# Sequence 0 of an attention-and-gate kernel: one pair of heads moved from float32 products to float16 parts, and one product of the first keys with two query blocks

## The chip, the cores and the metric

The kernel runs on one core of one Trainium2 chip. The core has five engines that run side by side and meet only through semaphores: TensorE (PE: matrix products, and its weight loads, PEld), VectorE (DVE), ScalarE (ACT), GpSimd (POOL) and SyncE (SP, which in this kernel issues every DMA). The metric is the device time of one execution in microseconds; lower is better. Times quoted as "the median" are over several executions; the profile is of one execution.

## The reference, cut to what matters

Eight sequences (B = 8) of 576 tokens, eight heads (H = 8) of width 64. Each head does causal softmax attention and a read of a linear memory; both are mixed by a gate per head. The result, 4608 x 512, goes through a two-layer net with the gate h * clip(h + 3, 0, 6) / 6.

```python
scores = scale * np.matmul(q, k.transpose(0, 1, 3, 2))
scores = np.where(causal, -1000000000.0, scores)
a = np.exp(scores - scores.max(-1, keepdims=True)); a /= a.sum(-1, keepdims=True) + 1e-09
local = np.matmul(a, v)
q_p = phi(q)                                   # elu(q) + 1
mem_out = (q_p @ M_prev) / (q_p @ z_prev + 1e-06)
attn = g * mem_out + (1 - g) * local
...
h = x @ w_in
out = (h * np.clip(h + 3.0, 0.0, 6.0) / 6.0) @ w_out
```

## The kernel before

**Tiling.** A sequence's 576 tokens are five query blocks (four of 128 and one of 64). Heads go in four pairs (p = 0 to 3). A `Unit` (L325) is one head of one pair for a group of query blocks; the groups are `UNITS` (L321): blocks 0 and 1 together (u = 0), then 2, 3 and 4 alone. A sequence has 32 units, in the order u, pair, head; unit t of sequence 0 with u = 0 has t = 0 to 7, so the last pair has t = 6 and 7, then 14 and 15, 22 and 23, 30 and 31. A unit does `scores` (PE: keys times queries, one product per key block j up to the query block, and the causal mask by another product), `reduce` (a maximum: DVE at L371, ACT for block 0, then an all-reduce over partitions on POOL at L373), `sub` (DVE, L379), `exp` (ACT, L386), `pv` (PE: the values, and the memory) and, after a pair's second head, `combine`.

**Two arithmetics.** For sequences 1 to 7 each operand is split into a float16 high and low part. `prep_steps` (L168) does that for a pair: three loads into staging tiles (tag stg, three buffers), sums of absolute values on ACT and an all-reduce on POOL, scales, then for k, q, phi(q) and v a `split` (L160: ACT writes the high part, DVE the low one). For k and phi(q) `stack` (L213) moves the parts by SBUF-to-SBUF DMAs, four for each, so that high and low lie on partitions 0 to 63 and 64 to 127; `do_q` issues four such DMAs too. The parts of k, q, phi and phi(q) come from a pool of three buffers (tag hl). `mem_steps` (L288) does the same for a sequence's memory. A score is then two products of float16 (L354, L355) and one mask (L361), a value product is three (L423 to L425), a memory product two per head (L427); POOL makes the high part of the weights (L390), DVE the low one (L398), and `combine` uses four ACT instructions a block (L455, L456) and one DVE add (L457).

For sequence 0 all four pairs are used as they are loaded, in float32 (`nat`): `nat_load` brings a pair in two parts, `nat_phi` makes phi(q) on ACT and DVE, a score is one float32 product on 64 partitions (L350), the mask is done by products with `selm` and `neg2` (L358), a value product is one float32 product (L416), the memory product of a pair is one (L418), and `combine` multiplies and adds on DVE (L446, L448). Each float32 product is two PE instructions in the trace, one of float16 is one.

**Slots.** Six slots (NSLOT) hold what a pair needs. The pairs of sequence 0 use slots 0 to 3, slots 4 and 5 are first the landing place for weights; `selm` and `neg2` lie at the tail of slot 3.

**The weights.** w_in and w_out come as 64-bit numbers, 16 loads of 1 MB (`w_load`). `w_decode` turns one into float32: ACT (L643), DVE (L644, L645), and a sum of absolute values on ACT (L646) that writes over the landing place, after which the next load may be issued into it. Block 0 of the net (256 tokens, `NNAT`) runs in float32 on these (L537, L563); then the weights are split in place (`w_split`), and the other 17 blocks run in float16 parts (L542 to L544, L565 to L567). Block 0 needs the rows of query blocks 0 and 1 of sequence 0 from all four pairs, which PE transposes (L524).

**The order.** `LOADS` (L40) is the order of the first loads: kind 0 and 1 are the two parts of a pair of sequence 0, 2 a weight load, 3 the memory. `B_T` (L41) says at which t the second part of each pair's phi is made. Every piece of work is given a due number (`due`, L736, `at`); a planner at compile time simulates the engines and lays down a fixed order for each engine from these numbers. At run time each engine goes through its own order and waits where an operand isn't there.

Of the kernel before, what the change touches and what calls it, by code (L numbers as in the profile page):

```python
# [28 lines left out]
SA = 256.0  # L29
TINY = 2.0 ** -40  # L30
NSLOT = 6
NNAT = 1

X_T = 10
# [2 lines left out]
W_AFTER = [3, 4, 5, 5, 6, 6, 7, 7] + [7] * 8  # L37
PSS, PSO = 3, 2

LOADS = ((0, 0), (3, 0), (0, 1), (0, 2), (0, 3), (2, 0), (2, 1), (1, 0), (1, 1), (2, 2), (1, 2), (1, 3), (2, 3))  # L40
B_T = (2, 3, 4, 5)  # L41
OF = (0,)
RMAX_STEPS = 3.0
LEAD = 40
# [24 lines left out]
def kernel(ctx, tc, qT, kT, v, mz, beta, w_in, w_out, out):  # L69
# [48 lines left out]
    for i in range(NSLOT):  # L118
        sizes = [2 * NB * P, 4 * S, 2 * S, NB * 2 * 129]
        whole = const.tile([P, sum(sizes) + 2], F16, name=f"slot{i}")  # L120
        at = 0
        for lst, n, pat, kw in zip((kst, qhl, qps, vst), sizes,
                                   ["p (h s) -> p h s", "p (x h s) -> p x h s", "p (h s) -> p h s",
                                    "p (t h e) -> p t h e"],
                                   [dict(h=2), dict(x=2, h=2), dict(h=2), dict(t=NB, h=2)]):
            lst.append(whole[:, at:at + n].rearrange(pat, **kw))
            at += n
        if i < NP:
            w32 = whole.bitcast(F32)
            nat.append(dict(q=w32[:, 0:S], k=w32[:, S:S + NB * P], qp=w32[:, S + NB * P:2 * S + NB * P],  # L130
                            v=w32[:, 2 * S + NB * P:2 * S + NB * P + NB * 130]
                            .rearrange("p (t h e) -> p t h e", t=NB, h=2)))
        else:
            raw.append(whole[:, 0:4096])
        if i == NP - 1:

            free = whole.bitcast(BF16)[:, 2 * (2 * S + NB * P + NB * 130):]
            selm = free[:, 0:2 * P].rearrange("p (a k) -> p a k", a=2)
            neg2 = free[:, 2 * P:3 * P].rearrange("p (a q) -> p a q", a=2)

    def at(step):

        tc.cur_priority = int(round(step * 1000))
# [24 lines left out]
    def prep_steps(b, p):  # L168
        sl = (NP * b + p) % NSLOT
        st = {}  # L170

        def pad(dst, value):
            if NP * b + p < NP + NSLOT:
# [20 lines left out]
        def scale():  # L194
            amr = st["amr"]
            ACT.activation(amr[:, 3:4], amr[:, 0:1], AF.Copy, bias=1.0)
            s, i = scales(amr, 4, TS, f"{b}_{p}")
            st["s"] = s
            scal = small.tile([P, 4], F32, name=f"scal_{b}_{p}", tag="scal", bufs=8)
            DVE.scalar_tensor_tensor(scal[:, 0:1], i[:, 0:1], 0.125, i[:, 1:2], op0=ALU.mult, op1=ALU.mult)  # L200
            DVE.memset(scal[:, 2:3], SA * 1e-9)
            ACT.activation(scal[:, 3:4], s[:, 3:4], AF.Copy, scale=mem[b]["eps1"])
            coef = mem[b]["coef"][:, 2 * p:2 * p + 2]
            ACT.activation(coef[:, :, 0], omg[:, 2 * p:2 * p + 2], AF.Copy, scale=i[:, 2:3])
            eps = scal[:, 2:4].unsqueeze(1).broadcast_to([P, 2, 2])
            esc = scal[:, 0:1]
            slots[b, p] = dict(sl=sl, esc=esc, coef=coef, eps=eps)
# [67 lines left out]
    def nat_mem():  # L275
        m = p2.tile([P, H * (D + 1)], F32, name="m_nat", tag="mz")
        DVE.memset(m, 0.0)
        m = m.rearrange("p (j h e) -> p j h e", h=2, e=D + 1)
        for r in range(2):
            SP.dma_start(m[D * r:D * r + D, :, r], mz[0].rearrange("d (j h) e -> d j h e", h=2)[:, :, r])  # L280
        coef = small.tile([P, H, 2], F32, name="coef_0", tag="coef", bufs=2)
        DVE.tensor_copy(coef[:, :, 0], omg)
        DVE.tensor_copy(coef[:, :, 1], gate)
        mem[0] = dict(t=m, coef=coef)
# [3 lines left out]
    def mem_steps(b):  # L288
        st = {}

        def load():
            t = st["t"] = stg.tile([P, NB * P], F32, name=f"stm_{b}", tag="stg")
            m = st["m"] = t[:, 0:H * (D + 1)].rearrange("p (h e) -> p h e", e=D + 1)
            for r in range(2):
                SP.dma_start(m[D * r:D * r + D], mz[b])

        def absmax():
            am = small.tile([P, 2], F32, name=f"amm_{b}", tag="amm", bufs=2)
            amr = st["amr"] = small.tile([P, 2], F32, name=f"ammr_{b}", tag="ammr", bufs=2)
            m = st["m"]  # L300
            abs_sum(am[:, 0:1], m[:, :, 0:D])
            abs_sum(am[:, 1:2], m[:, :, D:])
            POOL.partition_all_reduce(amr, am, P, RMAX)

        def conv():
            s, i = scales(st["amr"], 2, TS, f"m{b}")
            t = p2.tile([P, 2, H, D + 1], F16, name=f"mz_{b}", tag="mz")
            m = st["m"]
            split(t[:, 0, :, 0:D], t[:, 1, :, 0:D], m[:, :, 0:D], s[:, 0:1])
            split(t[:, 0, :, D:], t[:, 1, :, D:], m[:, :, D:], s[:, 1:2])  # L310
            coef = small.tile([P, H, 2], F32, name=f"coef_{b}", tag="coef", bufs=2)
            DVE.tensor_scalar(coef[:, :, 1], gate, s[:, 1:2], i[:, 0:1], op0=ALU.mult, op1=ALU.mult)
            eps1 = small.tile([P, 1], F32, name=f"eps1_{b}", tag="eps1", bufs=2)
            DVE.tensor_scalar_mul(eps1, s[:, 1:2], 1e-6)
            mem[b] = dict(t=t, s=s, coef=coef, eps1=eps1)

        return [load, lambda: None, absmax, conv]

# [6 lines left out]
    class Unit:  # L325
        def __init__(self, b, u, p, h):
            self.b, self.u, self.p, self.h = b, u, p, h
            self.blocks = []
            c = mcol = 0
            for i in UNITS[u]:  # L330
                self.blocks.append((i, rows[i], c, mcol))
                c += (i + 1) * rows[i]
                mcol += rows[i]
            self.n, self.m = c, mcol
            self.id = f"{b}_{u}_{p}_{h}"

        def scores(self):
            h = self.h
            if self.b == 0:
                t = nat[self.p]  # L340
            else:
                sl = slots[self.b, self.p]["sl"]
            sT = self.sT = ps_s.tile([P, 512], F32, name=f"sT_{self.id}", tag="sT")
            for i, nq, c0, _ in self.blocks:
                q0 = i * P
                for j in range(i + 1):
                    o = sT[:, c0 + j * nq:c0 + (j + 1) * nq]
                    if self.b == 0:
                        r = slice(D * h, D * h + D)
                        PE.matmul(o, t["k"][r, j * P:(j + 1) * P], t["q"][r, q0:q0 + nq],  # L350
                                  start=True, stop=j < i)
                    else:
                        kk = kst[sl][:, h, j * P:(j + 1) * P]
                        PE.matmul(o, kk, qhl[sl][:, 0, h, q0:q0 + nq], start=True, stop=False)  # L354
                        PE.matmul(o, kk, qhl[sl][:, 1, h, q0:q0 + nq], start=False, stop=j < i)  # L355
                    if j == i and self.b == 0:
                        for a in range(nq // D):
                            PE.matmul(o[:, a * D:(a + 1) * D], selm[r, a, :], neg2[r, a, :],  # L358
                                      start=False, stop=a == nq // D - 1)
                    elif j == i:  # L360
                        PE.matmul(o, ident16, negm[:, 0:nq], start=False, stop=True)  # L361
# [22 lines left out]
        def exp(self):  # L384
            a = self.a[:, 0:self.n]
            self.exp_ins = ACT.activation(a, a, AF.Exp, scale=slots[self.b, self.p]["esc"], bias=LN_SA)  # L386
            if self.b == 0:
                return
            self.ah = p2.tile([P, 512], F16, name=f"ah_{self.id}", tag="ah")
            POOL.affine_select(self.ah[:, 0:self.n], a, pattern=[[0, self.n]], compare_op=ALU.is_ge,  # L390
                               fill=0.0, base=1, channel_multiplier=0)

        def lo(self):
            if self.b == 0:
                return
            self.al = p2.tile([P, 512], F16, name=f"al_{self.id}", tag="al")
            n = self.n
# [1 line left out]

        def pv(self):  # L400
            b, p, h = self.b, self.p, self.h
            mt = mem[b]["t"]
            for i, nq, c0, _ in self.blocks:
                if h == 0:
                    if b == 0 and i in OF and i < 2:
# [5 lines left out]
                o, om = g[0:nq, h, 0, :], g[0:nq, h, 1, :]  # L411
                qs = slice(i * P, i * P + nq)
                cs = [slice(c0 + j * nq, c0 + (j + 1) * nq) for j in range(i + 1)]
                if b == 0:
                    for j in range(i + 1):
                        PE.matmul(o, self.a[:, cs[j]], nat[p]["v"][:, j, h, :], start=j == 0, stop=j == i)  # L416
                    if h == 1:
# [274 lines left out]
    DVE.memset(bias_g, TG / 2.0)  # L692
    DVE.memset(half, 0.5)
    DVE.memset(amx, 0.0)
    for p in range(NP):
        nat_pads(p)
    DVE.memset(nat_eps[:, 0:1], SA * 1e-9)
    DVE.memset(nat_eps[:, 1:2], 1e-6)
# [4 lines left out]
    for x, n in LOADS:  # L703
        if x < 2:
            nat_load(n, x)
        elif x == 2:
            w_load(n)
        else:
            nat_mem()
    am1 = const.tile([P, 8], F32, name="am1")  # L710
    am2 = const.tile([P, 8], F32, name="am2")
    for p in range(NP):
        nat_phi(p, 0)

    def w1_split():
# [45 lines left out]
    for t in range(NU + 2):  # L761
        if t < NU:
            u = units[t]
            if t % upb == 0 and u.b + 1 < B:
# [3 lines left out]
                for p, ks in enumerate(PREP_AT if t else PREP_AT_0):  # L768
                    for f, k in zip(ps[p], ks):
                        plan.setdefault(t + k, []).append(f)  # L770
        for p in range(NP):
            if t == B_T[p]:
                at(due(t) + PO)
                nat_phi(p, 1)
# [64 lines left out]
```

## Time and profile before

| what | us |
|---|---|
| median of 3 runs | 1101.2 (1100.18 to 1104.09) |
| the profiled execution, its own time | 1104.08 |
| its span, first to last instruction | 1102.4 |
| PE busy in the span | 1071.24 |
| DVE busy | 893.04 |
| ACT busy | 788.96 |
| POOL busy | 405.18 |

The profiled execution is at the upper end of the three runs; 1.7 us of its time lie outside its span. An engine's busy time is the union of its instructions. On PE the ends of matmuls are modelled, so what PE can do is read from the distance between the starts of like instructions rather than from their durations. The rows that matter are shown with the prediction.

### The profile page before, as it was taken

To read this page: it belongs to the slowest core of one execution; us is meant where nothing else is said; L and a number is where in the kernel's file an instruction comes from. 1 tells how busy PE (TensorE), PEld (TensorE's weight loads), DVE (VectorE), ACT (ScalarE), POOL (GpSimd) and SP (SyncE) were. 2 spreads that over 40 slices of the span, in tenths; PEclk is the share of its full clock that TensorE was granted. 3 is DMA by queue.
4 is the path that set the end of the run, shared out by engine and by line. 5 is a ranking of instruction groups with operands and counts; after the bars stand their busy time and mean duration, and the time that the engine had idled before them with its cause. 6 is when DMAs were issued, how large, how long until landed. Compare 5 with 4: busy or idle time off the path is not lost.

```text
span 1102.4 us, 28691 instructions
## 1 busy us (share of the span) xinstructions
PE 1071.2 (97%) x10728; PEld 788.6 (72%) x10728; DVE 893.0 (81%) x2350; ACT 789.0 (72%) x1884; POOL 405.2 (37%) x544
## 2 busy tenths in 40 slices
PE   7999999899999999999999999999999999999998
PEld 6888758586767776776768686768686858685664
DVE  5989779899899979998989896999699868792321
ACT  4778769778888878788877887778687857563322
POOL 2322123445455434533344533453244433350000
PEclk9999999999999999999999999999999999999999
DMA  8835452334333432443433432332432230101100
GB/s 251 313 110 174 108 148 78 77 85 102 102 97 97 98 106 78 117 92 101 103 102 47 136 99 51 81 102 76 128 82 68 52 77 14 29 10 31 30 10 20
DMA packets 101467, 101.38 MB, mean 92 GB/s; under 512 B 50256, under 2 KB 80976, under 8 KB 101328
## 3 DMA queue, kind: packets, MB, share of 16 engines
q1 hardware_dynamic: 101328, 99.56, 33.6%
q8 instruction: 84, 1.38, 0.6%
q14 instruction: 55, 0.45, 0.1%
HBM read 48.14 MB, written 9.44 MB: 52 GB/s over the span
## 4 chain that ended last, share of the span: by engine, by line
PE 39%; DVE 18%; ACT 5%; issue 5%; DMA 4%; POOL 1%; SPq 1%; DVEq 0%; ACTq 0%; POOLq 0%
PE po L565 6%; PE po L567 6%; PE po L566 6%; PE ph L542 5%; PE ph L543 5%; PE ph L544 5%; DVE rm L371 3%; DVE a L379 3%; DVE al L398 3%; DVE r L551 2%; DVE g L553 2%; PE sT L354 1%; PE sT L355 1%; PE o L425 1%; PE o L423 1%
## 5 line engine op out<-in xcount | busy, mean ns | idle before, releaser
L373 POOL PARTITION_ALL_REDUCE mb<-rm x256 | 253.9, 992 | 354.5 <-DVE rm L371 249.8
L542 PE MATMUL ph<-x,W 128*128 128x256 f16 x1088 | 296.6, 273 | 3.0 <-DMA x<-W 2.2
L543 PE MATMUL ph<-x,W 128*128 128x256 f16 x1088 | 296.6, 273 | 0.0
L544 PE MATMUL ph<-x,W 128*128 128x256 f16 x1088 | 296.6, 273 | 0.0
L565 PE MATMUL po<-W,g 128*128 128x512 f16 x544 | 206.2, 379 | 5.0 <-ACT ot L573 3.5
L567 PE MATMUL po<-W,g 128*128 128x512 f16 x544 | 206.2, 379 | 0.9 <-DVE g L553 0.9
L566 PE MATMUL po<-W,g 128*128 128x512 f16 x544 | 206.2, 379 | 0.0
L390 POOL TENSOR_SCALAR_AFFINE_SELECT ah<-a 128x384 f16<-128x384 f32 (+2 forms) x224 | 138.3, 619 | 183.0 <-ACT a L386 124.3
L386 ACT ACTIVATE a<-a,scal 128x384 f32<-128x384 f32 (+2 forms) x224 | 141.0, 631 | 63.1 <-DVE a L379 54.1
L379 DVE TENSOR_TENSOR a<-sT,mb 128x128 f32<-128x128 f32 (+3 forms) x320 | 148.3, 479 | 25.6 <-POOL mb L373 19.7
L398 DVE TENSOR_TENSOR al<-a,ah 128x384 f16<-128x384 f32 (+2 forms) x224 | 135.5, 605 | 10.7 <-POOL ah L390 9.9
L371 DVE TENSOR_REDUCE rm<-sT 128x128 f32<-128x256 f32 (+3 forms) x256 | 135.0, 527 | 8.3 <-ACT rm L369 3.8
L551 DVE SCALAR_TENSOR_TENSOR r<-r,ph 128x512 f32<-128x512 f32 x136 | 92.0, 677 | 52.5 <-ACT r L550 51.9
L550 ACT ACTIVATE r<-ph,bias_g,gsc 128x512 f32<-128x512 f32 x136 | 106.4, 783 | 33.2 <-PE ph L544 29.4
L355 PE MATMUL sT<-slot 128*128 128x128 f16 (+1 forms) x840 | 126.7, 210 | 0.0
L354 PE MATMUL sT<-slot 128*128 128x128 f16 (+1 forms) x840 | 124.2, 210 | 1.9 <-DVE a L379 1.4
L542 PEld LDWEIGHTS <-W 128*128 128x128 f16 x1088 | 106.4, 98 | 18.1 <-issue 3.0
L423 PE MATMUL o<-slot,ah 128*128 128x65 f16 (+1 forms) x840 | 116.1, 196 | 3.2 <-POOL ah L390 1.6
L543 PEld LDWEIGHTS <-W 128*128 128x128 f16 x1088 | 106.3, 98 | 15.7 <-issue 1.1
L424 PE MATMUL o<-slot,ah 128*128 128x64 f16 (+1 forms) x840 | 115.2, 195 | 0.0
L455 ACT ACTIVATE x<-o,cf 128x64 f32<-128x64 f32 (+1 forms) x280 | 88.0, 314 | 37.4 <-DVE cf L442 37.2
L544 PEld LDWEIGHTS <-W 128*128 128x128 f16 x1088 | 106.3, 98 | 11.7
(157 smaller groups left out, 2297.3 us busy)
## 6 DMA issues: line engine op xcount, KB each, us to landing
slot<-q SPq DMA_DIRECT2D x112, 144.0 KB, 2.5
out<-ot SPq DMA_DIRECT2D x36, 256.0 KB, 2.0
stv<-vn SPq DMA_DIRECT2D x28, 320.0 KB, 3.5
W<-w_in SPq DMA_DIRECT2D x8, 1024.0 KB, 11.2
slot<-w_out SPq DMA_DIRECT2D x8, 1024.0 KB, 5.0
stq<-qT SPq DMA_DIRECT2D x28, 288.0 KB, 3.1
stk<-kT SPq DMA_DIRECT2D x28, 288.0 KB, 3.2
slot<-k SPq DMA_DIRECT2D x112, 72.0 KB, 2.0
```

Source lines behind the costliest of these rows:

```text
L371: DVE.tensor_reduce(rm[:, m0:m0 + nq], src.rearrange("p (t q) -> p q t", q=nq), axis=AX.X, op=ALU.max)
L373: POOL.partition_all_reduce(mb[:, 0:self.m], rm[:, 0:self.m], P, RMAX)
L379: DVE.tensor_tensor(a[:, c0:c0 + w].rearrange("p (t q) -> p t q", q=nq), self.sT[:, c0:c0 + w].rearrange("p (t q) -> p t q", q=nq), self.m ...
L386: self.exp_ins = ACT.activation(a, a, AF.Exp, scale=slots[self.b, self.p]["esc"], bias=LN_SA)
L390: POOL.affine_select(self.ah[:, 0:self.n], a, pattern=[[0, self.n]], compare_op=ALU.is_ge, fill=0.0, base=1, channel_multiplier=0)
L398: DVE.tensor_tensor(self.al[:, 0:n], self.a[:, 0:n], self.ah[:, 0:n], op=ALU.subtract)
L542: PE.matmul(ph[:, m], wh, f["xh"][:, c], start=c == 0, stop=False)
L543: PE.matmul(ph[:, m], wh, f["xl"][:, c], start=False, stop=False)
L544: PE.matmul(ph[:, m], wl, f["xh"][:, c], start=False, stop=c == 3)
L565: PE.matmul(po, gh[:, m, ts], W2[:, m, 0:512], start=m == 0, stop=False)
L566: PE.matmul(po, gh[:, m, ts], W2[:, m, 512:], start=False, stop=False)
L567: PE.matmul(po, gl[:, m, ts], W2[:, m, 0:512], start=False, stop=m == 15)
```

## The change

The last pair of sequence 0 (p = 3) is no longer used in float32: it is loaded, split and stacked as the pairs of the later sequences are, and its units take the float16 branch in all but `combine`. Its `prep_steps` (that is, the steps after the load) and those of a `mem_steps(0)` are issued with the units t = 1 to 4, by the tables `PREP_0` and `MEM_0`, and their loads stand fourth in `LOADS` (kind 4). The memory of sequence 0 is therefore loaded twice, once in float32 for pairs 0 to 2 and once to be split; its landing place and its parts, and `selm` with `neg2`, lie in the unused tails of slots 0, 2 and 1.

For the pairs that stay in float32, the unit of blocks 0 and 1 does key block 0 in one product with 256 queries; before, there were two products with 128 queries each.

```diff
+NATP = 3
-LOADS = ((0, 0), (3, 0), (0, 1), (0, 2), (0, 3), (2, 0), (2, 1), (1, 0), (1, 1), (2, 2), (1, 2), (1, 3), (2, 3))
-B_T = (2, 3, 4, 5)
+LOADS = ((0, 0), (3, 0), (0, 1), (4, 3), (0, 2), (2, 0), (2, 1), (1, 0), (1, 1), (2, 2), (1, 2), (2, 3))
+B_T = (2, 3, 4)
+
+PREP_0 = (0, 0, 1, 1, 2, 2, 2, 3, 4, 4)
+MEM_0 = (0, 0, 1, 2)
...
-        if i < NP:
+        if i < NATP:
...
-        if i == NP - 1:
-
-            free = whole.bitcast(BF16)[:, 2 * (2 * S + NB * P + NB * 130):]
+        free = whole[:, 2 * (2 * S + NB * P + NB * 130):]
+        if i == 0:
+            m16_raw = free.bitcast(F32)[:, 0:H * (D + 1)]
+        elif i == 2:
+            m16 = free[:, 0:2 * H * (D + 1)].rearrange("p (x h e) -> p x h e", x=2, h=H)
+        elif i == 1:
+
+            free = free.bitcast(BF16)
             selm = free[:, 0:2 * P].rearrange("p (a k) -> p a k", a=2)
...
+        mk = b or "split"
...
-            ACT.activation(scal[:, 3:4], s[:, 3:4], AF.Copy, scale=mem[b]["eps1"])
-            coef = mem[b]["coef"][:, 2 * p:2 * p + 2]
+            ACT.activation(scal[:, 3:4], s[:, 3:4], AF.Copy, scale=mem[mk]["eps1"])
+            coef = mem[mk]["coef"][:, 2 * p:2 * p + 2]
...
+            t = stg.tile([P, NB * P], F32, name=f"stm_{b}", tag="stg")[:, 0:H * (D + 1)] if b else m16_raw
...
+            t = p2.tile([P, 2, H, D + 1], F16, name=f"mz_{b}", tag="mz") if b else m16
...
+            self.nat = b == 0 and p < NATP
...
-                    if self.b == 0:
-                        r = slice(D * h, D * h + D)
+                    if self.nat and self.u == 0 and j == 0:
+
+                        if i == 0:
+                            PE.matmul(sT[:, 0:2 * P], t["k"][r, 0:P], t["q"][r, 0:2 * P], start=True, stop=False)
+                    elif self.nat:
                         PE.matmul(o, t["k"][r, j * P:(j + 1) * P], t["q"][r, q0:q0 + nq],
                                   start=True, stop=j < i)
...
-                    if j == i and self.b == 0:
+                    if j == i and self.nat:
...
-            if self.b == 0:
+            if self.nat:
                 return
             self.ah = p2.tile([P, 512], F16, name=f"ah_{self.id}", tag="ah")
...
-            mt = mem[b]["t"]
+            mt = mem[b if self.nat else b or "split"]["t"]
...
-                if b == 0:
+                if self.nat:
...
-    for p in range(NP):
+    for p in range(NATP):
         nat_pads(p)
...
+        elif x == 4:
+            prep0 = prep_steps(0, n)
+            mem0 = mem_steps(0)
+            prep0[0]()
+            mem0[0]()
...
-    for p in range(NP):
+    for p in range(NATP):
         nat_phi(p, 0)
...
-        for p in range(NP):
+        for fs0, ks in ((mem0, MEM_0), (prep0, PREP_0)):
+            for f, k in zip(fs0[1:], ks[1:]):
+                if k == t:
+                    at(due(t))
+                    f()
+        for p in range(NATP):
             if t == B_T[p]:
```

`scores`, `exp`, `lo` and `pv` test `self.nat` now; `combine` keeps its test `b == 0`, so the last pair still goes through L446 and L448 there.

More of the change, by code (lines that the diff above doesn't have):

```diff
@@ L132 @@
                             .rearrange("p (t h e) -> p t h e", t=NB, h=2)))
-        else:
+        elif i >= NP:
             raw.append(whole[:, 0:4096])
-        if i == NP - 1:
-            free = whole.bitcast(BF16)[:, 2 * (2 * S + NB * P + NB * 130):]
+        free = whole[:, 2 * (2 * S + NB * P + NB * 130):]
[5 more added lines that the diff above has]
+            free = free.bitcast(BF16)
             selm = free[:, 0:2 * P].rearrange("p (a k) -> p a k", a=2)
@@ L280, in nat_mem @@
             SP.dma_start(m[D * r:D * r + D, :, r], mz[0].rearrange("d (j h) e -> d j h e", h=2)[:, :, r])
-        coef = small.tile([P, H, 2], F32, name="coef_0", tag="coef", bufs=2)
+        coef = small.tile([P, H, 2], F32, name="coef_n", tag="coef", bufs=3)
         DVE.tensor_copy(coef[:, :, 0], omg)
@@ L291, in load @@
         def load():
-            t = st["t"] = stg.tile([P, NB * P], F32, name=f"stm_{b}", tag="stg")
-            m = st["m"] = t[:, 0:H * (D + 1)].rearrange("p (h e) -> p h e", e=D + 1)
+            t = stg.tile([P, NB * P], F32, name=f"stm_{b}", tag="stg")[:, 0:H * (D + 1)] if b else m16_raw
+            m = st["m"] = t.rearrange("p (h e) -> p h e", e=D + 1)
             for r in range(2):
@@ L306, in conv @@
             s, i = scales(st["amr"], 2, TS, f"m{b}")
-            t = p2.tile([P, 2, H, D + 1], F16, name=f"mz_{b}", tag="mz")
+            t = p2.tile([P, 2, H, D + 1], F16, name=f"mz_{b}", tag="mz") if b else m16
             m = st["m"]
@@ L310, in conv @@
             split(t[:, 0, :, D:], t[:, 1, :, D:], m[:, :, D:], s[:, 1:2])
-            coef = small.tile([P, H, 2], F32, name=f"coef_{b}", tag="coef", bufs=2)
+            coef = small.tile([P, H, 2], F32, name=f"coef_{b}", tag="coef", bufs=3)
             DVE.tensor_scalar(coef[:, :, 1], gate, s[:, 1:2], i[:, 0:1], op0=ALU.mult, op1=ALU.mult)
@@ L314, in conv @@
             DVE.tensor_scalar_mul(eps1, s[:, 1:2], 1e-6)
-            mem[b] = dict(t=t, s=s, coef=coef, eps1=eps1)
+            mem[b or "split"] = dict(t=t, s=s, coef=coef, eps1=eps1)
         return [load, lambda: None, absmax, conv]
@@ L338, in scores @@
             h = self.h
-            if self.b == 0:
+            if self.nat:
                 t = nat[self.p]
+                r = slice(D * h, D * h + D)
             else:
@@ L386, in exp @@
             self.exp_ins = ACT.activation(a, a, AF.Exp, scale=slots[self.b, self.p]["esc"], bias=LN_SA)
-            if self.b == 0:
+            if self.nat:
                 return
@@ L393, in lo @@
         def lo(self):
-            if self.b == 0:
+            if self.nat:
                 return
@@ L413, in pv @@
                 cs = [slice(c0 + j * nq, c0 + (j + 1) * nq) for j in range(i + 1)]
-                if b == 0:
+                if self.nat:
                     for j in range(i + 1):
```

## The prediction

> **What bounds the kernel now.** I read the head of the page first, for the share of each engine, then the windows view with a stretch for each stage.
>
> ```profile
> span 1102.4 us, 28691 instructions
> PE 1071.2 (97%) x10728; PEld 788.6 (72%) x10728; DVE 893.0 (81%) x2350; ACT 789.0 (72%) x1884; POOL 405.2 (37%) x544
> ```
>
> ```profile
> 0.00:20.00 20.00, 14.91 (x79) 13.58 (x79) 10.40 (x62) 7.05 (x17) 5.82 (x14) 1.00 0.80 238
> 20.00:40.00 20.00, 16.54 (x76) 14.93 (x76) 16.71 (x46) 14.27 (x28) 5.46 (x4) 1.00 1.00 330
> 40.00:61.00 21.00, 20.88 (x90) 18.42 (x89) 16.64 (x44) 17.69 (x36) 6.61 (x8) 1.00 0.51 198
> 61.00:140.00 79.00, 79.00 (x486) 62.07 (x485) 69.60 (x174) 59.09 (x109) 17.33 (x21) 1.00 0.46 140
> 140.00:163.00 23.00, 20.52 (x104) 10.63 (x102) 15.85 (x43) 15.95 (x33) 6.62 (x6) 0.93 0.57 147
> 163.00:1102.40 939.40, 919.39 (x9905) 669.00 (x9903) 763.82 (x1985) 674.90 (x1663) 363.35 (x492) 1.00 0.30 76
> ```
>
> PE is idle for 31.2 us in all (1102.4 - 1071.2), and 8.5 of these lie in the first 40 us. From 40 us on PE is the bound, so a microsecond of PE work that goes from sequence 0 after that is a microsecond off the end, if nothing new makes PE wait. From 20 to 40 us the DMA share is 1.00 at 330 GB/s: the front is paced by loads. DVE is no light load either, 69.60 of 79 us in the fourth stretch.
>
> Second, the price of a PE instruction: the timeline of PE, read from start to start of neighbouring groups.
>
> ```profile
> 57.24 1.65 PE L350 MATMUL sT<-slot 64*128 64x128 f32 x6
> 58.69 0.31 PE L358 MATMUL sT<-slot 64*128 64x64 bf16 x2
> 58.92 1.54 PE L416 MATMUL o<-slot,a 128*128 128x65 f32 x6
> 60.26 0.74 PE L418 MATMUL o<-m_nat,slot 128*128 128x130 f32 x2
> 60.80 5.50 PE L537 MATMUL ph<-x,W 128*128 128x256 f32 x20
> ...
> 69.78 5.45 PE L537 MATMUL ph<-x,W 128*128 128x256 f32 x24
> ...
> 80.43 1.16 PE L350 MATMUL sT<-slot 64*128 64x128 f32 x8
> 81.42 0.22 PE L358 MATMUL sT<-slot 64*128 64x64 bf16 x2
> ...
> 99.69 1.00 PE L416 MATMUL o<-slot,a 128*128 128x65 f32 x8
> 100.53 0.44 PE L418 MATMUL o<-m_nat,slot 128*128 128x130 f32 x2
> 100.90 1.16 PE L350 MATMUL sT<-slot 64*128 64x128 f32 x8
> ```
>
> Before 60.8 us a float32 score instruction takes (58.69 - 57.24)/6 = 0.242 us, after it (81.42 - 80.43)/8 = 0.124; a value instruction (60.26 - 58.92)/6 = 0.223, then (100.53 - 99.69)/8 = 0.105. So PE runs at half pace until about 61 us and at full pace afterwards, though the windows give a granted clock of 1.00 in both. The step comes when the first long run of float32 products of the net starts (60.80).
>
> **The change part by part.** *PE work of the last pair.* Two heads; blocks 0 to 2 (t = 6, 7, 14, 15) have 12 products in the slow stretch, block 3 has 8 and block 4 has 10 in the fast one. The float16 forms stand in the timeline of sequence 1:
>
> ```profile
> 156.50 0.22 PE L361 MATMUL sT<-negm,ident 128*128 128x128 bf16 x1
> ...
> 157.23 0.22 PE L361 MATMUL sT<-negm,ident 128*128 128x128 bf16 x1
> ```
>
> ```profile
> 163.54 0.19 PE L423 MATMUL o<-slot,ah 128*128 128x65 f16 x1
> ...
> 163.93 0.27 PE L544 MATMUL ph<-x,W 128*128 128x256 f16 x1
> ```
>
> From the first to the second row there are 13 steps, 0.056 us each; from the third to the fourth 12, 0.033 each. Their price at the slow pace has no row: at least these, at most double, as for every float32 form; I take double (0.113 and 0.065).
>
> - Slow, a product: 2 x 0.242 + 2 x 0.223 = 0.93 becomes 2 x 0.113 + 3 x 0.065 = 0.42, so 0.51 x 12 = 6.1 us. Memory, three blocks: 0.54 (60.80 - 60.26) becomes 4 x 0.065, so 0.8. Masks: 12 of 0.115 (58.92 - 58.69 for two) become 6 of 0.113, so 0.7. Sum 7.6; with the fast prices for the new forms 10.2.
> - Fast, block 3: 2 x 0.124 + 2 x 0.105 = 0.46 becomes 0.21, so 2.0 for 8; memory 0.37 (100.90 - 100.53) becomes 0.13, so 0.2. Block 4 has 64 queries; a score of it takes 0.23 (ten starts in 1.17 us up to the mask):
>
> ```profile
> 137.12 1.32 PE L350 MATMUL sT<-slot 64*128 64x64 f32 x10
> 138.29 0.19 PE L358 MATMUL sT<-slot 64*128 64x64 bf16 x1
> ```
>
>  It becomes two of the short kind, 0.07, so 1.7 for 10; its values I count at no gain. Sum 3.9.
>
> *One product with 256 queries, six units.* Four instructions of 0.242 become two of 256 columns. At full pace these take 5.45/24 = 0.227, doubled 0.45, so 0.97 becomes 0.90: 0.4 us over six units; between 0 and 6 x 0.48 = 2.9 if only the weight load counted.
>
> Together PE loses 7.6 + 3.9 + 0.4 = **11.9 us** of work, of which 4.5 belong to blocks 0 and 1 (six products 3.1, memory 0.6, masks 0.5, the joined product 0.4). These fall where PE still waits for loads, in part: I count half, so 2.2 are lost again.
>
> *Loads.* Before the first part of pair 2 stand now 288 + 288 + 320 KB of the last pair and 2 x 130 KB of memory in place of 384 KB behind it: 772 KB, at 238 to 330 GB/s 2.3 to 3.2 us for everything behind. What is late today is late again: ScalarE already stands still at 21 us for the second part of a pair, and PE 2.3 us behind it.
>
> ```profile
> 21.10 0.47 ACT L268 ACTIVATE slot<-slot 128x320 f32<-128x320 f32 x1 [5.33 <-DMA slot<-qT]
> ...
> 23.23 0.76 PE L350 MATMUL sT<-slot 64*128 64x128 f32 x2 [2.26 <-issue]
> ```
>
> I take 2.5 us on the path; 0 at best (if the planner orders these later), 3.2 at worst.
>
> *The splitting.* DVE gets four low parts, the memory's two, and the low part of the weights of eight units; ACT three sums, the high parts and the memory; POOL eight selects and two reductions. Of DVE, from the groups by form:
>
> ```profile
> L398 DVE TENSOR_TENSOR al<-a,ah 128x384 f16<-128x384 f32 x112 | 67.8, 605 | 7.6 <-POOL ah L390 7.3
> L398 DVE TENSOR_TENSOR al<-a,ah 128x512 f16<-128x512 f32 x56 | 39.7, 708 | 0.8 <-POOL ah L390 0.7
> ...
> L163 DVE SCALAR_TENSOR_TENSOR k<-stk,s,k 128x576 f16<-128x576 f32 x28 | 23.5, 839 | 4.3 <-ACT k L162 4.2
> ```
>
> 2 x (0.605 + 0.605 + 0.708 + 0.55) = 4.9 (320 columns by the line through the other two), and some 5 for splits and scales (four near 0.84, the memory near 1.1, the rest small): 10 us, of which the splits fit into the 9.6 us that DVE idles in the first 20. The other cover is thin: from 61 to 140 us DVE idles 9.4 us; 2.5 more work (blocks 3 and 4) in a stretch 3.9 shorter leaves 3.0. PE's waits for DVE in the first 160 us are small now,
>
> ```profile
> PE sT L350 <- DVE a L379: 1.4, 2, 1.1
> ```
>
> and I count as much once more: 1.4 us; 0 at best, all of the fast gain (3.9) at worst. ACT's cover is wider (59.09 of 79). Without it its eight microseconds would count too.
>
> *Stacking.* Twelve SBUF-to-SBUF DMAs enter SP's queue, behind the loads of the list:
>
> ```profile
> 23.68 2.54 SPq L630 DMA_DIRECT2D W<-w_in  x1
> ```
>
> An issue of a stack takes SP 0.6 us, as one of sequence 1 shows:
>
> ```profile
> 107.89 0.60 SPq L215 DMA_DIRECT2D slot<-k  x1
> ```
>
> SP is through the list at 26.2 us, so the stacks cannot be issued much sooner unless the planner puts them ahead, whereas PE starts t = 6 at 23.23 now. Behind that start on PE stand values of earlier pairs and t = 7. The planner can put block 2 of the first pairs there, so I count nothing beyond the 2.5; the worst is the first rival.
>
> Sum: -11.9 + 2.2 + 2.5 + 1.4 = **-5.8 us**, from 1104.1 in the profiled execution to 1098.3. That execution is 2.9 above the median, so on the median's scale it is 1101.2 - 5.8 = **1095.4**.
>
> **The rivals.** *(a) Slower: PE waits for the stacks.* If the planner puts the two 1 MB weight loads that follow the list before the stacks, 6.2 us at 330 GB/s go ahead, and with eight issues of 0.6 the stacks of k and q are out near 37 us; the parts of phi(q), whose buffer frees only when those of k have been stacked, need a split (0.8 on ACT and on DVE), four issues and a landing more, some 5 us. PE, in order, then waits 37 - 23 + 5 = 19 us less the 11.9: +7, so **1108**. It decides from a wait of 11.9 us on, that is from stacks of which the last land after about 35. For it: the loads run at the DMA engines' limit from 20 to 40. Against: the order is planned, and six units of other pairs can go ahead.
>
> *(b) No change: DVE takes it.* If DVE is the bound from 61 to 140, the 3.9 go, and 1.7 more as al of blocks 0 to 2 comes late: -11.9 + 2.2 + 2.5 + 3.9 + 1.7 = -1.6, **1099.6**.
>
> *(c) Faster: the pace rises sooner.* What PE does at half pace takes half as long once the pace has doubled, so a step 14 us earlier, well inside the dense stretch from 40 us on, would bring 7 us on top: **1088**. It would need PE's float16 runs to count as busier than the float32 ones do. For it speaks that the step comes with a dense run; against it that 20.88 of 21 us were busy from 40 to 61, and a score still took 0.242. The Trainium skill, "TensorE: Matmul & The Clock Gate", Part 1, says that PE is at half clock until it has been busy for some 3.4 us; by that it would be fast from about 44 us on already, and this rival would have nothing left to bring. The trace disagrees with the page there.
>
> **How the numbers follow.** A measurement of this kernel can tell about 0.5% (5.5 us) from no change. That puts the border of faster at 1095.7, close to the forecast. Forecast (1091 to 1099, its own unknown costs) 0.48, of which 0.32 below the border, since most of the terms that I took as losses can be 0; (b) 0.23; (a) 0.16; (c) 0.13. Faster by over 0.5%: 0.32 + 0.13 = 0.45; within: 0.16 + 0.23 = 0.39; slower: 0.16. The range is 1085 (front hidden, c) to 1108 (a).
>
> **What would show it.** Right: 168 L350 instructions in place of 240 (14 products of two for each of six heads), and 30 L354 of sequence 0; the first long run of L537 no later than 61 us; FFN block 1 (L542) starting near 157 instead of 163; PE idle within 4 us of 31.2. Wrong: a wait of PE for a DMA of the last pair's slot between 20 and 40 us (a); DVE over 95% from 61 to 130 with PE waiting at L379 or L398 (b); a score of 0.124 us well before the first L537 (c).

## The result, and the profile after

The changed kernel takes **1134.7 us** (median of 4 runs, 1132.91 to 1137.93) against 1102.1 for the kernel before (1100.18 to 1104.09): a ratio of 1.030, interval 1.027 to 1.033. It is 3% slower. The forecast was 1095.4, and the time lies above the whole range (1085 to 1108). The profiled execution took 1132.91 us, of which 1131.2 are its span.

The head of the page after, with the share of each engine:

```profile
span 1131.2 us, 28825 instructions
PE 1063.8 (94%) x10748; PEld 777.5 (69%) x10748; DVE 904.0 (80%) x2373; ACT 795.4 (70%) x1901; POOL 410.3 (36%) x554
```

PE's work did fall, by 7.4 us (1071.2 to 1063.8). But PE is idle for 67.4 us instead of 31.2: 36.2 more. The sum, 28.8, is the difference of the spans. The windows view says where the idle time lies (columns as before: length, then the busy time of PE, PEld, DVE, ACT, POOL, then the granted clock, the DMA share, GB/s):

```profile
0.00:20.00 20.00, 11.20 (x54) 8.98 (x55) 9.15 (x59) 9.33 (x27) 5.50 (x15) 1.00 0.88 263
20.00:40.00 20.00, 11.04 (x45) 9.14 (x44) 19.09 (x58) 16.43 (x30) 4.10 (x3) 1.00 1.00 330
40.00:61.00 21.00, 4.06 (x25) 3.48 (x26) 4.34 (x14) 3.83 (x12) 1.44 (x2) 1.00 0.78 243
61.00:140.00 79.00, 72.81 (x449) 59.54 (x448) 73.12 (x169) 65.61 (x119) 27.40 (x30) 0.96 0.41 134
140.00:163.00 23.00, 23.00 (x181) 17.82 (x182) 19.85 (x70) 17.27 (x37) 7.53 (x11) 1.00 0.35 93
163.00:1131.20 968.20, 941.63 (x10000) 678.50 (x9998) 778.50 (x2009) 682.91 (x1679) 364.31 (x494) 1.00 0.30 76
```

Against the same stretches of before, PE idles 3.7 us more in the first, 5.5 in the second, 16.8 in the third, 6.2 in the fourth, 2.5 less in the fifth and 6.6 more in the rest. In the third **every** engine stands still (4.06, 4.34, 3.83 and 1.44 of 21 us busy), while the DMA engines are 0.78 busy: almost nothing computes until a transfer lands. PE's view of the waits names it (total, times, longest):

```profile
PE sT L370 <- DMA slot<-q: 18.2, 1, 18.2
PE o L431 <- ACT a L401: 6.7, 4, 2.9
```

One product (L370, the second half of the first score of the last pair; L355 before) waits 18.2 us for the stacks of q. SyncE's timeline shows why they come so late (start, length, operation; x is the number of issues):

```profile
27.88 3.04 SPq L233 DMA_DIRECT2D slot<-q  x2
...
37.87 1.56 SPq L645 DMA_DIRECT2D W<-w_in  x3
39.48 0.65 SPq L233 DMA_DIRECT2D slot<-q  x1
40.43 1.02 SPq L645 DMA_DIRECT2D W<-w_in  x1
41.51 0.78 SPq L233 DMA_DIRECT2D slot<-q  x1
```

Two of the four DMAs of q are issued at 27.9, the other two at 39.5 and 41.5. Three 1 MB loads of weights have just gone ahead of the third, a fourth ahead of the last, and the last lands at 56.8, 15.3 us after its issue. So the wait is rival (a) of the prediction, with the stacks 20 us later than it assumed.

What L370 itself reads had landed long before. The first two DMAs are those of the first head, and each brings the high and the low part for one half of the partitions; L369, which ran at 38.33 on all 128 partitions, needed both of them, and L370 reads the low part that came in the same two. It waits for the *second* head's DMAs. In the tile the parts lie in the order high of head 0, high of head 1, low of head 0, low of head 1, so that, taken as one range of addresses, a DMA of the second head spans the first head's low part. That this range is the reason is argued from the code: e3 below makes the ranges disjoint, but the order of issue changes with it.

PE's timeline holds a second thing:

```profile
38.33 0.26 PE L369 MATMUL sT<-slot 128*128 128x128 f16 x1 [1.58 <-DMA slot<-q]
56.80 0.29 PE L370 MATMUL sT<-slot 128*128 128x128 f16 x1 [18.22 <-DMA slot<-q]
...
57.10 0.31 PE L370 MATMUL sT<-slot 128*128 128x128 f16 x1
57.21 0.31 PE L369 MATMUL sT<-slot 128*128 128x128 f16 x1
...
73.23 2.82 PE L431 MATMUL o<-slot,a 128*128 128x65 f32 x12
75.85 0.74 PE L433 MATMUL o<-m_nat,slot 128*128 128x130 f32 x2
...
80.25 2.04 PE L552 MATMUL ph<-x,W 128*128 128x256 f32 x4 [0.28 <-DVE z L461]
82.09 1.67 PE L431 MATMUL o<-slot,a 128*128 128x65 f32 x12
83.59 0.44 PE L433 MATMUL o<-m_nat,slot 128*128 128x130 f32 x2
```

A float16 score starts every 0.11 us at 57, and a float32 value takes (75.85 - 73.23)/12 = 0.218 at 73: PE is **still at half pace**, where before it had been at full pace since 61. The first L552 (L537 before), the net's block 0, which needs the last pair, starts at 80.25, and full pace comes right behind it: a value then takes (83.59 - 82.09)/12 = 0.125 us. The window from 61 to 82:

```profile
61.00:82.00 21.00, 17.59 (x97) 14.99 (x96) 19.90 (x48) 17.13 (x28) 11.63 (x10) 1.00 0.14 47
```

PE did 17.6 us of work there that would have taken about half as long at full pace. That is an estimated 8.8 us, and without them its work would have fallen by 16.

### The profile page after: what moved, and what is told of

It reads as the page before. It is cut to its first block, busy times and chain, and to the rows that moved or that the text cites. A ratio compares the mean times of both kernels' runs of the same rounds, so it can differ in the third digit from the quotient of the medians.

```text
span 1131.2 us, 28825 instructions
## 1 busy us (share of the span) xinstructions
PE 1063.8 (94%) x10748; PEld 777.5 (69%) x10748; DVE 904.0 (80%) x2373; ACT 795.4 (70%) x1901; POOL 410.3 (36%) x554
## 4 chain that ended last, share of the span: by engine, by line
PE 34%; DVE 8%; ACT 4%; issue 3%; DMA 3%; POOL 1%; SPq 1%; DVEq 0%; ACTq 0%; POOLq 0%
PE po L580 5%; PE po L581 5%; PE po L582 5%; PE ph L557 4%; PE ph L558 4%; PE ph L559 4%; DVE al L413 1%; DVE a L394 1%; PE sT L369 1%; PE o L438 1%; PE sT L370 1%; DVE rm L386 1%; PE o L440 1%; DVE g L568 1%; DVE r L566 1%
## 5 line engine op out<-in xcount | busy, mean ns | idle before, releaser
L388 POOL PARTITION_ALL_REDUCE mb<-rm x256 | 250.5, 979 | 326.7 <-DVE rm L386 236.6
L405 POOL TENSOR_SCALAR_AFFINE_SELECT ah<-a 128x384 f16<-128x384 f32 (+2 forms) x232 | 146.0, 631 | 210.3 <-ACT a L401 121.1
L401 ACT ACTIVATE a<-a,scal 128x384 f32<-128x384 f32 (+2 forms) x232 | 145.7, 629 | 49.2 <-DVE a L394 41.1
L394 DVE TENSOR_TENSOR a<-sT,mb 128x128 f32<-128x128 f32 (+3 forms) x320 | 148.2, 478 | 16.8 <-POOL mb L388 15.0
L386 DVE TENSOR_REDUCE rm<-sT 128x128 f32<-128x256 f32 (+3 forms) x256 | 134.8, 527 | 22.4 <-ACT rm L384 19.5
L413 DVE TENSOR_TENSOR al<-a,ah 128x384 f16<-128x384 f32 (+2 forms) x232 | 142.0, 612 | 12.5 <-POOL ah L405 11.7
L370 PE MATMUL sT<-slot 128*128 128x128 f16 (+1 forms) x870 | 133.9, 211 | 18.2 <-DMA slot<-q 18.2
L369 PE MATMUL sT<-slot 128*128 128x128 f16 (+1 forms) x870 | 133.1, 211 | 4.1 <-DVE a L394 2.1
L438 PE MATMUL o<-slot,ah 128*128 128x65 f16 (+1 forms) x870 | 122.2, 196 | 12.8 <-POOL ah L405 6.7
L439 PE MATMUL o<-slot,ah 128*128 128x64 f16 (+1 forms) x870 | 120.9, 195 | 0.0
L567 ACT ACTIVATE g<-r 128x512 f16<-128x512 f32 x136 | 86.3, 635 | 47.5 <-DVE r L566 47.5
```

What stands on the lines that cost most here:

```text
L386: DVE.tensor_reduce(rm[:, m0:m0 + nq], src.rearrange("p (t q) -> p q t", q=nq), axis=AX.X, op=ALU.max)
L388: POOL.partition_all_reduce(mb[:, 0:self.m], rm[:, 0:self.m], P, RMAX)
L394: DVE.tensor_tensor(a[:, c0:c0 + w].rearrange("p (t q) -> p t q", q=nq), self.sT[:, c0:c0 + w].rearrange("p (t q) -> p t q", q=nq), self.m ...
L413: DVE.tensor_tensor(self.al[:, 0:n], self.a[:, 0:n], self.ah[:, 0:n], op=ALU.subtract)
```

## The experiments

All runs in one table; each ratio is to the kernel before, run on the same chip (its medians there lie between 1102.1 and 1103.7). PE's work and idle time are of one profiled execution each; executions of the kernel before alone spread from 1095.1 to 1105.9 us, so a few us of idle time between two profiles are no proof by themselves.

| run | median (runs) | ratio, interval | PE work | PE idle |
|---|---|---|---|---|
| before | 1101.2 (3) | | 1071.2 | 31.2 |
| after | 1134.7 (4) | 1.030 (1.027 to 1.033) | 1063.8 | 67.4 |
| e1_join_only | 1102.6 (12) | 1.002 (1.000 to 1.004) | 1072.5 | 29.5 |
| e2_split_only | 1134.7 (4) | 1.030 (1.027 to 1.034) | 1066.8 | 64.5 |
| e3_q_by_part | 1124.1 (4) | 1.020 (1.017 to 1.023) | 1067.6 | 53.2 |
| e4_decode_free | 1124.8 (4) | 1.021 (1.018 to 1.024) | 1060.9 | 62.3 |
| e5_wout_behind | 1124.1 (4) | 1.021 (1.017 to 1.024) | 1067.1 | 55.2 |
| e6_pair_later | 1108.4 (9) | 1.006 (1.004 to 1.008) | 1067.2 | 40.6 |
| e7_dense_run | 1104.7 (12) | 1.004 (1.002 to 1.006) | 1066.2 | 36.9 |
| e8_both | 1133.7 (4) | 1.030 (1.026 to 1.034) | 1069.7 | 59.1 |
| e9_later_dense | 1114.7 (4) | 1.011 (1.009 to 1.012) | 1067.0 | 47.6 |
| e10_order_only | 1120.2 (4) | 1.015 (1.013 to 1.018) | 1082.5 | 37.5 |
| e11_load_later | 1113.3 (5) | 1.009 (1.008 to 1.011) | 1067.8 | 42.6 |
| e12_dense_gap | 1127.6 (6) | 1.024 (1.021 to 1.027) | 1089.0 | 40.6 |

### Which half of the change: e1 and e2

e1 is the kernel before with the joined product alone; e2 is the kernel after without it:

```diff
-                    if self.nat and self.u == 0 and j == 0:
-
-                        if i == 0:
-                            PE.matmul(sT[:, 0:2 * P], t["k"][r, 0:P], t["q"][r, 0:2 * P], start=True, stop=False)
-                    elif self.nat:
+                    if self.nat:
```

> The kernel before with the joined product (256 queries) alone; all four pairs stay in float32. Theory A (the loss comes from the last pair's stacks of q, which land at 56.8 us while PE waits from 38.6): no stacks here, so within 2 us of before, at best 1 us faster. Rival C (the joined product or the order that follows from it costs the time): clearly slower than before, 10 us or more.

> The changed kernel with two products of 128 queries again, so the split of the last pair alone. Theory A: the same wait of PE for the stacks of q, 15 to 20 us, and 1132 to 1138 us in all. Rival C: close to before, 1100 to 1110.

The joined product alone changes nothing that can be told; without it the kernel after is as slow as with it. The whole loss belongs to the split pair.

### The wait for the stacks: e3 and e5

`do_q` moves one half of the partitions of high and low part in one DMA. For the last pair e3 makes two of it, one for each part. On top of that e5 holds back two 1 MB loads of w_out until the last stack of q is issued.

```diff
                 for r in range(2):
+                    if b == 0:
+                        for x in range(2):
+                            SP.dma_start(qhl[sl][D * r:D * r + D, x, h], t[D * h:D * h + D, x])
+                        continue
                     SP.dma_start(qhl[sl][D * r:D * r + D, :, h], t[D * h:D * h + D])
```

> The changed kernel with the last pair's four stacks of q made into eight, one for each part, so that those of one head no longer overlap the other's in the tile's address range; on SP all eight then stand before the loads of sequence 1 and of the weights 4 to 7. Theory A (two of the four q stacks stood behind these loads in SP's queue and behind 4 MB in the DMA engines): PE's wait at the last pair's first score falls from 18 to under 5 us, the time falls by 13 to 18, to 1117 to 1122. Rival D (DMA engines are full until 56 us whatever the order, so the wait moves to another place): 1130 or more.

> As e3_q_by_part, and the first two w_out loads (2 MB, not needed before 53 us) are issued only after the last pair's stacks. If what is left of the loss in e3 (22 us above before) is the place of the stacks behind loads: the stacks land some 6 us earlier, PE starts the last pair at about 31 instead of 37 and the time falls by 4 to 7, to about 1118. If it is the work of ScalarE and VectorE for the split in the first 40 us, which keeps PE waiting for the units before: under 3 us change.

In e3 PE's waits for stacks of k and q at the last pair's start fall from 18.2 to 3.3 us (1.8 for k at 37.30, 1.5 for q at 39.84), and the time falls by 10.6, not by the 15 of the wait and not by the 13 to 18 expected. The waits view of e3 shows what is late next:

```profile
PE sT L373 <- DVE a L398: 7.9, 8, 3.3
PE o L435 <- ACT a L405: 6.3, 4, 2.9
```

It is now the vector side: L398 (L379 before) takes the maximum off a score, L405 (L386) is the exponential. These are totals of the whole run: of the 7.9 us one wait of 3.3 lies in the first 160 us, and after has 6.7 us of the second kind already. In the windows from 20 to 40 us DVE is 18.53 of 20 us busy and PE 10.76. The net's first four instructions, at 67.20, do not end PE's half pace; it lasts until a run of 16 at 79.20. In e5 the last pair's first score starts at 32.06 instead of 37.30, yet the time is that of e3: those two loads aren't what remains.

### The decodes that wait for the last pair: e4 and e8

From the fifth weight load on, the decodes of ACT are tied to the units t = 6 and 7 by the table W_AFTER, so that ACT and DVE stood still with PE. e4 ties them to t = 5, with the 18 us wait as it was; e8 is e3 and e4 together.

```diff
-W_AFTER = [3, 4, 5, 5, 6, 6, 7, 7] + [7] * 8
+W_AFTER = [3, 4, 5, 5, 5, 5, 5, 5] + [5] * 8
```

> The changed kernel with the weight decodes from number 4 on tied to the exp of t = 5 and not to those of t = 6 and 7 (the last pair). Theory A: PE waits for the stacks of q as before; ScalarE and VectorE fill their idle time from 45 to 58 us with decodes, which brings the net's block 0 forward by a few us: 1122 to 1134. Rival B (the loss is the decode that hangs on the late pair): most of it comes back, 1110 or less.

> e3_q_by_part and e4_decode_free in one. If the two remove different losses: 1124 less 10, about 1114. If each removes the same loss (the time at which the weights of block 0 of the net are decoded): 1120 to 1125.

e4's windows, third stretch:

```profile
40.00:61.00 21.00, 3.58 (x23) 2.96 (x23) 14.46 (x22) 14.87 (x25) 1.51 (x2) 1.00 0.95 295
```

PE still waits (19.0 us for the same stacks), but ACT does 14.87 us of work there and DVE 14.46, and the time falls by 10 us. So about a third of the loss goes when the other engines may work on behind PE's wait, with the wait itself left as long as it was.

e8 takes both obstacles away and is as slow as after, above both of its ranges. Its windows say why not all is gained:

```profile
72.00:86.00 14.00, 10.90 (x86) 9.14 (x85) 12.72 (x31) 12.31 (x26) 5.80 (x6) 1.00 0.61 223
86.00:96.00 10.00, 9.56 (x42) 8.48 (x43) 9.55 (x18) 6.39 (x10) 1.95 (x2) 0.52 0.68 224
```

PE idles for 3.1 us between 72 and 86, and the granted clock then falls to 0.52 for 10 us. e8's PE work is 8.8 us more than e4's; its mean granted clock is 0.989, e4's 0.997, and 0.008 of 1128.8 us is 9.0. That is about PE's extra work. The idle time is only 3.2 below e4's though the long wait is gone: 11.1 less from 40 to 61 us, but 3.5 more from 61 to 100 and 6.3 more from 200 to 800. What causes the late part stays open.

### The place of the last pair: e6, e10 and e11

e6 is e3 with the last pair's units t = 6 and 7 moved behind those of query block 2 of the first two pairs. e10 makes the same move **in the kernel before**, where nothing is split. e11 is e6 with the last pair's and the memory's loads put behind the first part of pair 2.

```diff
+    late = units[6:8]
+    units = units[0:6] + units[8:12] + late + units[12:]
     NU = len(units)
```

> As e3_q_by_part, with the last pair's unit of blocks 0 and 1 moved behind the units of block 2 of pairs 0 and 1 (four units), so that PE has work of other pairs while the last pair is prepared; the decodes tied to t = 6 and 7 then hang on units of pair 0. If PE's fixed order at the last pair is what costs it: PE idle from 20 to 40 us falls from 9 to under 5 us and the time falls by 5 to 12, to 1112 to 1119. If block 0 of the net, which needs the last pair, sets the time: no gain, 1122 or more.

> The kernel before, nothing split, with only the last pair's two units of blocks 0 and 1 moved behind the third block's units of the first two pairs. If the 6 us that remain in the kernel with the moved pair are the price of the order, this one is 3 to 8 us slower than before (1105 to 1110), because block 0 of the net, which needs that pair, begins later. If they are the price of the splitting, it is within 3 us of before (1099 to 1105).

> The kernel with the moved pair, with the last pair's loads and the memory's second load put behind the first part of pair 2. That kernel's PE idles 8.5 us in the first 20, the kernel before 5.1. If the 2.5 us that the prediction counted for loads are on the path, this one is 2 to 4 us faster than the kernel with the moved pair: 1104 to 1106.5. If the time is given back later, as with the dense run, it stays at 1107 to 1110.

e6 is 15.7 us faster than e3, more than the 5 to 12 expected. Its PE does 17.86 us of work from 20 to 40 where e3 does 10.76: there are now products ahead of the stacks. e10 is the surprise. Moving the pair costs 1.5% (some 17 us, where 3 to 8 were expected) by itself, although PE hardly waits:

```profile
40.00:61.00 21.00, 21.00 (x95) 18.89 (x95) 19.36 (x47) 17.90 (x36) 7.74 (x8) 1.00 0.52 196
61.00:80.00 19.00, 19.00 (x87) 17.25 (x87) 18.77 (x49) 15.40 (x29) 5.97 (x6) 1.00 0.56 194
```

PE is busy all the time from 40 to 80, with a granted clock of 1.00 in the record. But its work has grown by 11.3 us with not one product more than before. Its timeline:

```profile
79.73 1.81 PE L416 MATMUL o<-slot,a 128*128 128x65 f32 x8
81.33 0.74 PE L418 MATMUL o<-m_nat,slot 128*128 128x130 f32 x2
81.87 2.83 PE L537 MATMUL ph<-x,W 128*128 128x256 f32 x10
...
88.31 1.00 PE L416 MATMUL o<-slot,a 128*128 128x65 f32 x8
89.15 0.44 PE L418 MATMUL o<-m_nat,slot 128*128 128x130 f32 x2
```

A value takes (81.33 - 79.73)/8 = 0.200 us ahead of the L537 at 81.87, and (89.15 - 88.31)/8 = 0.105 behind it. Block 0 of the net needs the last pair; its first long run, which ends the half pace, comes at 81.87 instead of 60.80. So the order's price is 11.3 us of half pace and 6.3 of idle time.

With **the same order**, the split kernel (e6) is 1.006 and the unsplit one (e10) 1.015: the splitting itself gains 0.9%, some 10 us. PE's work falls by 15.4 us (1082.5 to 1067.2), its idle time rises by 3.1. e6's own remaining loss, 6 us, is less than what its order costs.

e11 was to show the 2.5 us that the prediction counted for loads. It lies above both of its ranges: at 1.009, against e6's 1.006, it is no faster, and in its first 20 us PE does 11.38 us of work, e6 11.54. Taking those bytes away from ahead of pair 2 brings nothing back. After's timelines of ACT and DVE show what holds PE up there:

```profile
13.62 0.63 ACT L167 ACTIVATE junk<-slot 128x512 uint8<-128x512 f32 x1 [2.94 <-DMA slot<-mz]
15.29 0.42 DVE L280 SCALAR_TENSOR_TENSOR slot<-slot 128x256 f32<-128x256 f32 x1 [4.83 <-ACT slot L279]
```

ACT waits 2.9 us for the memory's second load, DVE stands still for 4.8 us behind ACT, and PE then waits 2.6 us for DVE. (The trace names L158, a scale of that memory; the L394 just ahead of it, which reads a score and so frees its buffer, is the likelier cause.) e11 makes that load later still: its ACT waits 4.2 us for it, and PE 1.9 for DVE at L398 and 1.6 for ACT at L405. So e11 took the bytes away and lengthened this wait, and doesn't tell the two apart.

### The pace by itself: e7, e9 and e12

Six float32 products of 256 columns, whose result is not used, are added to PE: in e7 to the kernel before ahead of the ninth unit, in e9 to e6 at the same place, in e12 to the kernel before ahead of the seventh unit, where PE stood still for 2.3 us.

```diff
+            if t == 8:
+                dn = ps_f.tile([P, 2, TB], F32, name="dense", tag="h")
+                for m in range(6):
+                    PE.matmul(dn[:, m % 2], ident, nat[0]["q"][:, 0:TB], start=True, stop=True)
             units[t].scores()
```

> The kernel before with six extra float32 products of 256 columns (results unused) ahead of the scores of t = 8, at about 31 us: a dense run of 5 us on PE at half pace. If a dense run is what brings the full pace, and it lasts while units follow: score instructions of the units from 36 us on take 0.12 instead of 0.24 us, and the time stays within 3 us of before or falls by up to 5. If the pace falls back between units, or has another cause: still 0.24 until 61 us, and 3 to 5 us slower.

> The kernel with the last pair's units moved behind (1108.4 us), plus the six float32 products of 256 columns (4.0 us of PE) ahead of the ninth unit, which raised PE's pace from half to full at once in the kernel before. Theory 'supply': from 20 to 80 us DVE is busy 57.4 of 60 us there, so a faster PE only waits more: 1106 to 1112, PE's idle time up by 5 or more. Rival 'pace': PE's half pace until 79 us is what remains: PE does some 32 us of work between 40 and 79 us, at full pace half of it, so 4 to 12 us less: 1096 to 1104.

> The kernel before with the same six float32 products of 256 columns, now ahead of the seventh unit, where PE stands still from 20.97 to 23.23 us: 2.3 of their 4.0 us fill that gap. Theory 'given back': the front is fed by loads and by DVE, and time won on PE there comes back later as PE's waits, as with the run ahead of the ninth unit: 1100 to 1105 us. Rival 'pace': PE does about 33 us of work at half pace between 25 and 61 us in the kernel before; if half of the gain stays, the kernel is 6 us or more faster: below 1097. Third: PE at full pace runs dry between 25 and 40 us, where loads pace it, the granted clock falls to 0.50 there, and the gain is lost that way: 1102 to 1110 with 0.50 in the windows.

e7, PE's timeline:

```profile
30.64 4.04 PE L787 MATMUL dense<-slot,ident 128*128 128x256 f32 x12
34.61 0.93 PE L350 MATMUL sT<-slot 64*128 64x128 f32 x6
35.38 0.22 PE L358 MATMUL sT<-slot 64*128 64x64 bf16 x2
```

Behind the run a score takes (35.38 - 34.61)/6 = 0.128 us instead of 0.242, and stays there. So the step at 60.80 in the kernel before is a matter of what PE runs, not of when. PE's work falls by 5.1 us, although the run itself adds 4.0. But PE's idle time grows by 5.7, nearly all of it (5.5) between 400 and 800 us, and the time isn't better (1.004). What takes the lead away again so late wasn't tried.

e12 is 2.4% **slower**. The fall of the clock in its third expectation came, but the price is far above the 1102 to 1110 given there. Its windows:

```profile
20.00:32.00 12.00, 10.35 (x54) 8.45 (x53) 6.79 (x17) 7.82 (x17) 2.13 (x2) 1.00 1.02 333
32.00:46.00 14.00, 10.79 (x48) 9.72 (x49) 11.50 (x35) 9.18 (x20) 4.81 (x5) 0.51 1.04 363
46.00:72.00 26.00, 26.00 (x106) 22.09 (x105) 24.84 (x66) 23.32 (x46) 8.17 (x8) 0.50 0.39 138
72.00:86.00 14.00, 14.00 (x87) 11.96 (x86) 12.84 (x25) 9.45 (x16) 2.67 (x3) 0.96 0.69 243
```

The run ends at 25.8; PE, now fast, soon has nothing to do, and the granted clock is 0.51 from 32 on. It stays at 0.50 through 26 us in which PE is busy without a gap, until the net's first run of ten instructions (69.62). PE's work is 17.8 us more than before's, of which 4.9 are the run itself. e9, which lies above both of its ranges too, has the same fall, from 45 to 85 us, and shows that 0.50 in the record and the half pace of the start are the same pace. Its timeline, float16 scores before and after the fall:

```profile
40.25 0.22 PE L373 MATMUL sT<-slot 128*128 128x128 f16 x1
40.30 0.22 PE L374 MATMUL sT<-slot 128*128 128x128 f16 x1
...
54.14 0.31 PE L374 MATMUL sT<-slot 128*128 128x128 f16 x1
54.25 0.31 PE L373 MATMUL sT<-slot 128*128 128x128 f16 x1
```

0.055 us at a granted 1.00, 0.11 at 0.50. And 0.11 is what after shows at 57 us, with 1.00 in the record.

No version beat the kernel before. The joined product alone (e1), the dense run (e7) and the moved pair (e6) come closest.

## Why the prediction was wrong

**The step that failed** is the one on stacking: "The planner can put block 2 of the first pairs there, so I count nothing beyond the 2.5". It did not: PE came to the last pair's products at 38 and waited there until 56.8. So the term for stacking, put at nothing, was a wait of 18.2 us. e6, which puts block 2 there by hand, takes 15.7 us off e3; e3, which only lets q's stacks come out earlier, takes 10.6 off after.

**Rival (a)** named the mechanism and priced it at a wait of 19 us, of which 12 would be paid for by the shorter work, hence 1108. The wait came out at 18.2, and that the two are so close is chance: the rival's wait ran from 23 to 42 and ended with the parts of phi(q), the measured one from 38.6 to 56.8 and ended with q. What it left out is what a wait does besides: the decodes on ACT and DVE stopped too (e4: 10 us), and block 0's net came 20 us later, which prolonged PE's half pace by 8.8 us of work (e10: 11.3 for the same delay with nothing split). It also placed the last stacks near 37 us, behind two weight loads; they came behind four more, and the two DMAs of the second head were issued 12 us after the first head's.

**"From 40 us on PE is the bound, so a microsecond of PE work that goes ... is a microsecond off the end, if nothing new makes PE wait"**: with the same order (e6 against e10) 15.4 us of work gave 12.2 us of span; in e7 5.1 gave nothing. It held in part, and no better than in part.

**PE's work.** The sum was 11.9 us; e6 against e10 gives 15.4, and after without its prolonged half pace 16. The slow price of the float16 forms, taken as double without a row, is about that: 0.11 against 0.055 for a score (e9). So the sum was too small, not too large. (Its side figure of 10.2, for the slow part with the fast prices of the new forms, comes to 10.9 from its own rows; the sum doesn't use it.) A likely reason, not shown by itself, is that more of the last pair's work stood in the half-pace stretch than the prediction put there. The 0.4 of the joined product can't be told (e1).

**Loads, 2.5 us, and DVE, 1.4.** PE did lose 3.7 us in the first 20. In the trace of after 2.6 of these are the wait behind DVE and ACT, which stood behind the memory's second load; e11 didn't bring them back, but it delayed that load too, so the share of the bytes stays open. DVE's share was larger than counted: in the first 160 us of after PE waits 4.2 us for L394 (2.2, 1.0 and 1.0), where before it waited 2.0 for the same line (L379, 1.4 and 0.6): 2.2 more, where 1.4 were counted.

**Rival (c)**, the pace rising sooner, was a real mechanism without its price: float16 runs did not raise the pace, a delayed net kept it down, and a run that did raise it early gave nothing (e7) or cost 2.4% (e12). Of the signs listed in the prediction two decided: the wait of PE for the last pair's slot between 20 and 40 us, which is rival (a), began at 38.6, and "the first long run of L537 no later than 61 us" came at 80 or later.

The Trainium skill, "TensorE: Matmul & The Clock Gate", Part 1, has the half clock as the resting state, released by some 3.4 us of busy PE and coming back after about as long an idle window. The trace agrees that there are two paces. On the release it differs: e12's PE was busy for 26 us of 26 at 0.50, and e10's for 40 of 40 from 40 to 80 us at half pace; in each it ended within a run of ten float32 instructions of 256 columns. On the return it differs too: e12's clock fell at 32 us, after an idle gap of 1.7, and e9's at 45, with no gap above 0.6 in the 5 us before.

## What to carry to other kernels

Before putting work that needs a chain of transfers on an engine that runs in order, look at what else waits behind its first product: here the late stacks stopped three engines and, by delaying the net's first dense run, kept PE at half pace for 20 us more. Price a delay of the first dense run as half of all PE work that it leaves in front of it (an extra run put in early brought nothing here, e7 and e12), and read the pace from the distance between starts of like instructions, for the granted clock read 1.00 here at both paces. Look, too, at which transfer a late product waits for: here it was not the one that brought its operand. An experiment that makes the suspected move in the unchanged kernel (e10) told the order's price from the splitting's, which the changed kernel alone could not.

## What the hardware showed that was not expected

- In the kernel before too, a short idle spell is followed by the slow clock (windows):

```profile
140.00:144.00 4.00, 1.88 (x25) 1.35 (x22) 2.10 (x7) 2.03 (x4) 0.52 (x1) 1.00 0.83 173
144.00:148.00 4.00, 3.63 (x5) 1.65 (x6) 3.74 (x12) 2.12 (x6) 1.48 (x2) 0.59 0.73 151
```

 PE idles 2.1 us of 4, and the granted clock of the next 4 us is 0.59. There long products of the net follow and it is over after some 5 us; in e9 and e12, with short products behind the fall, it lasted about 40.
- Being busy was not enough to raise the pace: products of 64 rows or 65 columns kept PE 100% busy at half pace. Wherever PE came at half pace to a run of 10 to 28 instructions of float32 products with 128 rows and 256 columns, full pace came during it (in e4, at 86.46, with its first instruction), and in e6 it came behind a run of six (79.39). The net's first runs, of four, mostly did not (e3 at 67.20, e4 at 79.79, e6 at 72.81, e10 at 67.17 and 77.92). In e8 (68.94) and after (80.25) full pace came right behind one, and in e2, which is after without the joined product, it did not (79.90). So the count by itself is not the rule, and what the rule is wasn't tried further.
